# A clustered attention whose loop over units is put together in twos

## The chip, the cores and the metric

The kernel runs on one core of one Trainium2 chip. The metric is the device time of one execution in microseconds; the number quoted for the kernel before is the median of three runs. A core has a matrix engine (TensorE, PE in the rows; PEld is its loading of weights), a vector engine (VectorE, DVE), a scalar engine (ScalarE, ACT), a general engine (GpSimd, POOL) and an engine that issues DMAs (SyncE, SP). Each takes its instructions in the order in which the program emits them; they meet through semaphores, which the framework derives from the tiles that they read and write.

## The reference

Three stages follow one another. Only the first is touched by the change. It is an attention over B = 2 batches, 8 heads, 768 positions and 64 columns a head, in which a query sees only the keys of its own cluster:

```python
q_assign = np.argmax(np.einsum('bhsd,hcd->bhsc', q_n, c_n), axis=-1)
k_assign = np.argmax(np.einsum('bhsd,hcd->bhsc', k_n, c_n), axis=-1)
mask = q_assign[:, :, :, None] == k_assign[:, :, None, :]
scores = scale * np.matmul(q, k.transpose(0, 1, 3, 2))
scores = np.where(mask, scores, -1000000000.0)
scores = scores - np.max(scores, axis=-1, keepdims=True)
attn = np.exp(scores)
attn = attn / (np.sum(attn, axis=-1, keepdims=True) + 1e-09)
return np.matmul(attn, v).astype(np.float32)
```

Then comes a mixture of 8 experts (each token goes to the one with the largest gate, through two matrices of 512x1024 and 1024x512 with a ReLU between), and last a bilinear layer, `(x @ w_a) * (x @ w_b) @ w_out` with an inner width of 1536.

## The kernel before

**Units.** The attention works on eight pairs of heads, one after the other (`p`, 0 to 7). A pair has 2 x 6 blocks of 128 queries, so twelve units (`NU = 12`), 96 in all. A unit takes 128 queries of one head against all 768 keys. Position m in this document is a unit's place in its pair of heads, 0 to 11.

**What a unit does.** `emit_s` computes its scores: four matmuls (512, 256, 512 and 256 columns) into a PSUM tile of two banks, tag `S`, of which there are two; VectorE then reduces them to the negated row maximum (L464). `emit_exp` has ScalarE take the exponential out of that same PSUM tile and sum the rows (L471). `emit_t` turns the probabilities with TensorE: six transposes of 128x128 (L485), three into each of the two banks of tag `T`; the first three are copied to SBUF by ScalarE (L489), the other three by VectorE (L491). The scores of unit i+2 so wait for the exponential of unit i, and the transposes of a unit for the copies of the unit before it.

**Values.** Each six units give a group whose values are computed by `pv_steps`, a generator: three blocks of four matmuls (L501) into the one bank of tag `O`, one block at every second step; behind the third ScalarE copies the result (L508), and one or two steps later `emit_x` turns it back with three matmuls (L529, tile `xo`) into the one bank of tag `X`, which VectorE reads in four operations, the last of them at L542.

**Preparation of the next pair of heads.** `STEPS` gives steps of class `Prep` a place in the loop. All their matmuls use the same single bank of tag `X`, so the next of them waits until the copies out of the one before are done. By position m: m = 10 turns the two halves of the raw queries (`turn`, L344, tiles `xq`, each copied out by ScalarE at L320), the first at "10 minus a half", ahead of the unit's transposes, the second behind them; m = 11 and m = 0 turn the keys (`xk`); m = 1 multiplies with the centroids (`sims`, L352, tile `sm`); m = 3 turns the similarities (`best`, L362, tile `st`; two VectorE operations read it); m = 4 makes the one-hot rows; m = 6 (again "minus a half") turns those of the queries and m = 7 those of the keys (`rows`, L384, tiles `otq` and `otk` with the pair's number; each is copied out by two ScalarE casts at L319 and two VectorE casts at L324).

**The loop.** One iteration i emits, on every engine in this order: scores of unit i, the steps of the values and then the steps planned at i minus a half, transposes of unit i-2 (`LAG = 2`), exponential of unit i, the steps planned at i. Nothing reorders them afterwards. Two iterations in a row put these blocks on TensorE: scores, values, transposes, scores, transposes, with the blocks of `X` between them.

Of the kernel before, what the change touches and what calls it, by code (L numbers as in the profile page):

```python
# [29 lines left out]
def cluster_attention__then__moe__then__bilinear_kernel(  # L30
# [183 lines left out]
    pairs = [(b, hp) for b in range(B) for hp in range(HP)]  # L214
# [5 lines left out]
    def load(p, names):  # L220
        b, hp = pairs[p]
        ts = loaded.setdefault(p, {})
        for src, nm in ((q, "qn"), (k, "kn"), (v, "vn")):
            if nm not in names:
                continue
            if nm == "vn":
                t = ap.tile([128, 2, NT, D], F32, tag=nm, name=f"{nm}{p}", bufs=2)
                nc.sync.dma_start(
                    out=t.rearrange("p h t d -> p h (t d)"),
                    in_=src[b, 2 * hp:2 * hp + 2].rearrange("h (p t) d -> p h (t d)", t=NT),  # L230
                )
            else:
                t = ap.tile([128, NT * 2 * D], F32, tag=nm, name=f"{nm}{p}", bufs=2)
                if p == 0:
                    t = t.rearrange("p (h t d) -> p h t d", h=2, t=NT)
                    nc.sync.dma_start(
                        out=t.rearrange("p h t d -> p h (t d)"),
                        in_=src[b, 2 * hp:2 * hp + 2].rearrange("h (p t) d -> p h (t d)", t=NT),
                    )
                    ts[nm] = t  # L240
                    continue
                t = t.rearrange("p (t h d) -> p t h d", t=NT, h=2)
                for h in range(2):
                    nc.sync.dma_start(
                        out=t[:, :, h, :],
                        in_=src[b, 2 * hp + h].rearrange("(p t) d -> p t d", t=NT),
                    )
            ts[nm] = t
# [204 lines left out]
    def emit_s(u):  # L453
        p, g, h, j = units[u]
        s, t = p % 2, NG * g + j
        if (g, h, j) == (0, 0, 0):
            sums[p] = ap.tile([128, NT, 2], F32, tag="sums", name=f"sums{p}", bufs=2)
        sc = ps.tile([128, 1024], F32, tag="S", name=f"s{u}", bufs=2)
        for i in range(2):
            w = qs[s, h][:, i, 128 * t:128 * t + 128]  # L460
            for c0, c1 in ((0, 512), (512, S)):
                nc.tensor.matmul(sc[:, c0:c1], lhsT=w, rhs=ks[s, h][:, i, c0:c1], start=(i == 0), stop=(i == 1))  # L462
        nm = ap.tile([128, 1], F32, tag="nm", name=f"nm{u}", bufs=3)
        nc.vector.tensor_reduce(out=nm, in_=sc[:, 0:S], axis=AX.X, op=ALU.max, negate=True)  # L464
        return sc, nm

    def emit_exp(u, sc, nm):
        p, g, h, j = units[u]
        pr = ap.tile([128, S], F32, tag="prob", name=f"pr{u}", bufs=3)
        t = NG * g + j  # L470
        nc.scalar.activation(out=pr, in_=sc[:, 0:S], func=AF.Exp, bias=nm, scale=1.0,  # L471
                             accum_out=sums[p][:, t, h:h + 1])
        prob[u] = pr

    def emit_t(u):
        p, g, h, j = units[u]
        pr = prob.pop(u)
        if (p, g, h) not in pt_t:
            pt_t[p, g, h] = ap.tile([128, NT, GN], F32, tag=f"pt{h}", name=f"pt{u}", bufs=2)
        pt = pt_t[p, g, h]  # L480
        for i in range(2):
            x = ps.tile([128, 512], F32, tag="T", name=f"t{u}{i}", bufs=2)
            for n in range(3):
                kb = 3 * i + n
                nc.tensor.transpose(x[:, 128 * n:128 * n + 128], pr[:, 128 * kb:128 * kb + 128], ident)  # L485
            dst = pt[:, 3 * i:3 * i + 3, 128 * j:128 * j + 128]
            src = x[:, 0:GN].rearrange("p (n c) -> p n c", n=3)
            if i == 0 or u >= len(units) - 2:
                nc.scalar.copy(out=dst, in_=src)  # L489
            else:  # L490
                nc.vector.tensor_copy(dst, src)  # L491

    def pv_steps(p, g, j0=0, nj=NG, tags=("O", "X"), per=1, spread=False):


        vn = loaded[p]["vn"]
        n = 128 * nj
        o = ps.tile([128, 512], F32, tag=tags[0], name=f"o{p}{g}{j0}")
        for kb in range(NT):
            for h in range(2):  # L500
                nc.tensor.matmul(o[64 * h:64 * h + 64, 0:n], lhsT=vn[:, h, kb, :],  # L501
                                 rhs=pt_t[p, g, h][:, kb, 128 * j0:128 * j0 + n],
                                 start=(kb == 0), stop=(kb == NT - 1))
            if kb < NT - 1 and kb % per == per - 1:
                for _ in range(per if spread else 1):
                    yield
        ot = ap.tile([128, GN], F32, tag="ot", name=f"ot{p}{g}{j0}", bufs=2)
        nc.scalar.copy(out=ot[:, 0:n], in_=o[:, 0:n])  # L508
        t0 = NG * g + j0
        sm = ap.tile([128, NG, 2], F32, tag="sm", name=f"sm{p}{g}{j0}", bufs=2)  # L510
        nc.vector.tensor_scalar(out=sm[:, 0:nj], in0=sums[p][:, t0:t0 + nj, :], scalar1=1e-9, scalar2=None, op0=ALU.add)
        nc.vector.reciprocal(out=sm[:, 0:nj], in_=sm[:, 0:nj])
        yield
        if spread:
            yield
        if g == 1 and p < LAST - 1:
            yield
        emit_x(p, t0, nj, ot, sm, tags[1])
        yield
# [264 lines left out]
    NU = 12  # L784
    LAG = 2
# [43 lines left out]
    cq, ck = p0.rows("q", "T", 2), p0.rows("k", "O", 1)  # L829
# [73 lines left out]
    end = NU * len(pairs)  # L903
# [33 lines left out]
                             stop=(t == NP - 1 and d % 2 == 1 and i == 1), skip_group_check=True)  # L937

    pvs = []
    for i in range(end + LAG):  # L940
        if i < end:
            sc_nm = emit_s(i)
            if i == 0:
                cq((1,))
                ck((1,))
            if i % NU == 1 and i // NU + 2 < len(pairs):
                load(i // NU + 2, ("qn", "kn"))
            if i % NU == 6 and i // NU + 1 < len(pairs):
                load(i // NU + 1, ("vn",))
        for st in pvs[::-1]:  # L950
            next(st, 0)
        for f in plan.get(i - 0.5, ()):
            f()
        if i == end - 1:
            next(tails[0])
        if i >= end - 1:
            next(r1[0])
        if i == end + 1:
            nc.sync.dma_start(out=x0, in_=xs[0:W].rearrange("(a p) d -> p a d", p=128))
        if i == end:  # L960
            next(tails[0])
            next(tails[1])
            next(r1[1])
        if i == end + 1:
            next(r1[1])
            next(tails[1])
            next(r1[2])
        if i >= LAG:
            emit_t(i - LAG)
        if i < end:  # L970
            emit_exp(i, *sc_nm)
        if i >= LAG:
            p, g, h, j = units[i - LAG]
            if (h, j) == (1, NG - 1) and (p, g) != (LAST, 1):
                last = (p, g) == (LAST, 0)
                pvs.append(pv_steps(p, g, per=3 if last else 2, spread=not last))
                pvs = pvs[-2:]
        for f in plan.get(i, ()):
            f()
        if i == end - 2:  # L980
            next(r1[0])
    next(tails[2])
    next(r1[2])
    place_mm(0, 0)
# [486 lines left out]
```

## Time and profile before

| | |
|---|---|
| median of three runs | 783.31 us (782.85 to 784.54) |
| time of the profiled execution | 783.25 us |
| its span, first to last instruction | 781.1 us |
| mean granted TensorE clock | 0.994 of 2.4 GHz |
| TensorE busy | 761.6 us, 98% of the span |
| VectorE, ScalarE, GpSimd busy | 67%, 46%, 20% |

"Busy" counts an instruction from its start to its modelled end, and matmuls overlap: how long TensorE really takes over a block of instructions is read from the start of one block to the start of the next. Below, a block has its letter in the tile that it writes: `s` scores, `t` transposes, `o` values, `xo`, `xq`, `xk`, `sm`, `st`, `ot5q` and `ot5k` the others. A row merges the instructions of a block (x6: six), its first number is the start of the first, its second the time to the modelled end of the last. A row of the view of windows has the stretch, its length, then the busy time and number of instructions of PE, PEld, DVE, ACT and POOL, the granted clock, the busy share of the DMA engines and the GB/s that they moved.

### The profile page before, as it was taken

Reading aid. Unit: us, or ns where it says so; the run is one execution under the profiler, and the core shown is the slowest. Engines: PE = TensorE matmul, PEld = TensorE weight load, DVE = VectorE, ACT = ScalarE, POOL = GpSimd, SP = SyncE. Lnnn points to the kernel's source line nnn. Section 1 sums busy time; section 2 is a strip of 40 time slices with the busy share of each in tenths; the row PEclk is TensorE's granted clock in tenths of the full one; section 3 lists DMA queues with packets and bytes.
Section 4 is the critical chain, followed back from the end, with each engine's and each line's share of the span. In section 5 each row is a group of like instructions: output and inputs, shape, how many; then the busy total and the mean of one; then the engine's idle time right before and its main releaser. Section 6 shows DMA issues by size and latency. Waiting matters only on the chain. (4 is left out here: it accounts for less than half of the span.)

```text
span 781.1 us, 12589 instructions
## 1 busy us (share of the span) xinstructions
PE 761.6 (98%) x4731; PEld 629.9 (81%) x4731; DVE 523.2 (67%) x947; ACT 355.6 (46%) x677; POOL 156.9 (20%) x164
## 2 busy tenths in 40 slices
PE   9999999999999999999999998999999999999996
PEld 8676676665766789998999997888888888888885
DVE  5867868778687778877686686766456765625323
ACT  6767666675666447547575432323132121210100
POOL 7623221415110410000007000211212112102011
PEclk9999999999999999999999999999999999999999
DMA  6685955737410168858789854322222220001011
GB/s 144 143 192 180 277 134 117 170 92 198 108 49 1 43 215 272 267 173 270 255 275 158 229 166 111 111 79 81 81 55 82 56 80 0 1 1 55 0 55 54
DMA packets 76302, 98.17 MB, mean 126 GB/s; under 512 B 28368, under 2 KB 49360, under 8 KB 76240
## 3 DMA queue, kind: packets, MB, share of 16 engines
q1 hardware_dynamic: 73792, 91.01, 42.2%
q0 software_dynamic: 2304, 6.31, 2.2%
q8 instruction: 38, 0.62, 0.4%
q14 instruction: 24, 0.20, 0.1%
q10 hardware_dynamic: 144, 0.03, 0.0%
HBM read 70.32 MB, written 10.50 MB: 103 GB/s over the span
## 5 line engine op out<-in xcount | busy, mean ns | idle before, releaser
L1408 PE MATMUL ab<-yh,hi 128*128 128x512 f32 x288 | 113.0, 392 | 0.0
L1408 PE MATMUL ab<-yh,lo 128*128 128x512 f32 x288 | 112.6, 391 | 0.0
L1415 DVE TENSOR_TENSOR ga<-ga,ab 128x512 f32<-128x512 f32 x36 | 24.7, 686 | 127.8 <-PE ab L1408 102.1
L464 DVE TENSOR_REDUCE nm<-s 128x1 f32<-128x768 f32 x96 | 91.5, 953 | 18.1 <-PE s L462 14.0
L145 DVE TENSOR_TENSOR lo<-raw,hi 128x1024 fp32r<-128x1024 f32 x70 | 84.8, 1223 | 22.4 <-ACT hi L139 21.7
L471 ACT ACTIVATE pr<-s,nm 128x768 f32<-128x768 f32 x96 | 87.0, 906 | 18.4 <-DVE nm L464 17.9
L462 PE MATMUL s<-ks,qs 128*128 128x512 f32 (+1 forms) x384 | 91.6, 361 | 0.3 <-ACT pr L471 0.3
L1414 ACT COPY ga<-ab 128x512 f32<-128x512 f32 x36 | 21.1, 586 | 151.9 <-PE ab L1408 151.9
L485 PE MATMUL t<-ident,pr 128*128 128x128 f32 x576 | 82.8, 277 | 3.8 <-DVE pt L491 2.2
L485 PEld LDWEIGHTS t<-ident,pr 128*128 128x128 f32 x576 | 64.6, 141 | 25.1 <-issue 10.8
L139 ACT CAST hi<-raw 128x1024 fp32r<-128x1024 f32 x70 | 72.2, 1048 | 17.4 <-DMA raw<-in_moe_w 17.3
L145 POOL TENSOR_TENSOR lo<-tmp,hi 128x512 fp32r<-128x512 f32 x28 | 38.2, 1365 | 204.6 <-ACT hi L139 204.6
L1408 PE MATMUL ab<-yl,hi 128*128 128x512 f32 x288 | 77.0, 389 | 0.0
L501 PE MATMUL o<-pt,vn 128*64 128x384 f32 (+1 forms) x432 | 74.5, 468 | 0.0
L491 DVE COPY pt<-t 128x384 f32<-128x384 f32 x94 | 51.8, 551 | 27.2 <-PE t L485 27.0
L489 ACT COPY pt<-t 128x384 f32<-128x384 f32 x98 | 46.7, 478 | 46.5 <-PE t L485 46.0
L462 PEld LDWEIGHTS s<-ks,qs 128*128 128x128 f32 x384 | 58.5, 190 | 9.6 <-issue 4.4
L1127 PE MATMUL y<-hh,hi 128*128 128x256 f32 x224 | 63.8, 285 | 0.0
L1408 PEld LDWEIGHTS ab<-yh,hi 128*128 128x128 f32 x288 | 54.5, 189 | 11.4
L1408 PEld LDWEIGHTS ab<-yh,lo 128*128 128x128 f32 x288 | 54.5, 189 | 11.3
L1408 PEld LDWEIGHTS ab<-yl,hi 128*128 128x128 f32 x288 | 54.1, 188 | 11.2
L1127 PE MATMUL y<-hh,lo 128*128 128x256 f32 x224 | 62.9, 281 | 0.0
(328 smaller groups left out, 1543.4 us busy)
## 6 DMA issues: line engine op xcount, KB each, us to landing
raw<-in_moe_w SPq DMA_DIRECT2D x72, 512.0 KB, 4.8
raw<-in_moe_w_a SPq DMA_DIRECT2D x12, 512.0 KB, 3.7
raw<-in_moe_w_b SPq DMA_DIRECT2D x12, 512.0 KB, 3.7
raw<-in_moe_w_out SPq DMA_DIRECT2D x12, 512.0 KB, 3.4
qs<-hiq SPq DMA_DIRECT2D x14, 384.0 KB, 4.8
ks<-hik SPq DMA_DIRECT2D x28, 192.0 KB, 4.8
xs<-zero SPq DMA_DIRECT2D x8, 512.0 KB, 5.5
xw<-xs SPq DMA_DIRECT2D x14, 256.0 KB, 5.0
```

Source lines behind the costliest of these rows:

```text
L139: nc.scalar.copy(out=hi, in_=raw)
L145: eng.tensor_tensor(out=lo, in0=raw, in1=hi.bitcast(F32), op=ALU.subtract)
L462: nc.tensor.matmul(sc[:, c0:c1], lhsT=w, rhs=ks[s, h][:, i, c0:c1], start=(i == 0), stop=(i == 1))
L464: nc.vector.tensor_reduce(out=nm, in_=sc[:, 0:S], axis=AX.X, op=ALU.max, negate=True)
L471: nc.scalar.activation(out=pr, in_=sc[:, 0:S], func=AF.Exp, bias=nm, scale=1.0, accum_out=sums[p][:, t, h:h + 1])
L485: nc.tensor.transpose(x[:, 128 * n:128 * n + 128], pr[:, 128 * kb:128 * kb + 128], ident)
L489: nc.scalar.copy(out=dst, in_=src)
L491: nc.vector.tensor_copy(dst, src)
L501: nc.tensor.matmul(o[64 * h:64 * h + 64, 0:n], lhsT=vn[:, h, kb, :], rhs=pt_t[p, g, h][:, kb, 128 * j0:128 * j0 + n], start=(kb == 0), sto ...
L1127: nc.tensor.matmul(y[:, d, 0:n], lhsT=a_[:, fb % 2, 128 * d:128 * d + 128], rhs=b_[:, 0:n], start=(fb == 0 and d % 2 == 0 and i == 0), sto ...
L1408: nc.tensor.matmul(p_, lhsT=a_[:, d, f0:f0 + 128], rhs=b_[d], start=(i == 0), stop=(i == len(seq) - 1))
L1415: nc.vector.tensor_tensor(out=ga, in0=ga, in1=ab[1], op=ALU.mult)
```

## The change

From iteration 4 up to iteration 83, two iterations i (even) and i+1 are emitted together: scores of i, scores of i+1, exponential of i, transposes of i-2, the values of step i with the steps planned at i minus a half, the steps planned at i, exponential of i+1, the values of step i+1, transposes of i-1, the steps planned at i+1. The other iterations (0 to 3 and 84 to 97) are as they were, but for the transposes and the exponential, which are in functions of their own now. No instruction is added or taken away, no tile gets another size or another number of buffers.

```diff
@@ -937,20 +937,27 @@
                              stop=(t == NP - 1 and d % 2 == 1 and i == 1), skip_group_check=True)
 
     pvs = []
-    for i in range(end + LAG):
-        if i < end:
-            sc_nm = emit_s(i)
-            if i == 0:
-                cq((1,))
-                ck((1,))
-            if i % NU == 1 and i // NU + 2 < len(pairs):
-                load(i // NU + 2, ("qn", "kn"))
-            if i % NU == 6 and i // NU + 1 < len(pairs):
-                load(i // NU + 1, ("vn",))
+    sc = {}
+
+    def do_s(i):
+        if i >= end:
+            return
+        sc[i] = emit_s(i)
+        if i == 0:
+            cq((1,))
+            ck((1,))
+        if i % NU == 1 and i // NU + 2 < len(pairs):
+            load(i // NU + 2, ("qn", "kn"))
+        if i % NU == 6 and i // NU + 1 < len(pairs):
+            load(i // NU + 1, ("vn",))
+
+    def do_pv(i):
         for st in pvs[::-1]:
             next(st, 0)
         for f in plan.get(i - 0.5, ()):
             f()
+
+    def do_tails(i):
         if i == end - 1:
             next(tails[0])
         if i >= end - 1:
@@ -965,20 +972,50 @@
             next(r1[1])
             next(tails[1])
             next(r1[2])
+
+    def do_t(i):
         if i >= LAG:
             emit_t(i - LAG)
+
+    def do_exp(i):
         if i < end:
-            emit_exp(i, *sc_nm)
+            emit_exp(i, *sc.pop(i))
+
+    def do_end(i):
         if i >= LAG:
             p, g, h, j = units[i - LAG]
             if (h, j) == (1, NG - 1) and (p, g) != (LAST, 1):
                 last = (p, g) == (LAST, 0)
                 pvs.append(pv_steps(p, g, per=3 if last else 2, spread=not last))
-                pvs = pvs[-2:]
+                del pvs[:-2]
         for f in plan.get(i, ()):
             f()
         if i == end - 2:
             next(r1[0])
+
+    i = 0
+    while i < end + LAG:
+        if 2 * LAG <= i < end - NU and i % 2 == 0:
+
+            do_s(i)
+            do_s(i + 1)
+            do_exp(i)
+            do_t(i)
+            do_pv(i)
+            do_end(i)
+            do_exp(i + 1)
+            do_pv(i + 1)
+            do_t(i + 1)
+            do_end(i + 1)
+            i += 2
+            continue
+        do_s(i)
+        do_pv(i)
+        do_tails(i)
+        do_t(i)
+        do_exp(i)
+        do_end(i)
+        i += 1
     next(tails[2])
     next(r1[2])
     place_mm(0, 0)
```

On TensorE, around m = 10 of one pair of heads (`xq`, `xk`: the raw queries and keys of the next pair; `t`, `s`: transposes and scores of a unit), the kernel before has

```order
L344 MATMUL xq_1697<-ident,qn_1421 128x128 x3
L485 MATMUL t_1702<-ident,pr_1654 128x128 x3
L485 MATMUL t_1707<-ident,pr_1654 128x128 x3
L344 MATMUL xq_1714<-ident,qn_1421 128x128 x3
L462 MATMUL s_1719<-ks_102,qs_101 128x512
...
L485 MATMUL t_1727<-ident,pr_1682 128x128 x3
L485 MATMUL t_1732<-ident,pr_1682 128x128 x3
L344 MATMUL xk_1739<-ident,kn_1424 128x128 x3
```

and the changed kernel

```order
L501 MATMUL o_1658<-pt_1464,vn_1197 64x384
L344 MATMUL xq_1716<-ident,qn_1387 128x128 x3
L344 MATMUL xq_1721<-ident,qn_1387 128x128 x3
L485 MATMUL t_1729<-ident,pr_1663 128x128 x3
L485 MATMUL t_1734<-ident,pr_1663 128x128 x3
L344 MATMUL xk_1739<-ident,kn_1390 128x128 x3
```

The transposes of one unit no longer stand between the two halves of the queries, and between the second half and the keys only one unit's transposes are left, without scores.

On TensorE, around m = 2 and 3 of the next pair of heads (`xo`: the values turned back; `st`: the similarities turned), the kernel before has

```order
L529 MATMUL xo_1834<-iw,ot_1758 128x144 x3
L485 MATMUL t_1844<-ident,pr_1773 128x128 x3
L485 MATMUL t_1849<-ident,pr_1773 128x128 x3
L462 MATMUL s_1861<-ks_98,qs_97 128x512
...
L485 MATMUL t_1868<-ident,pr_1811 128x128 x3
L485 MATMUL t_1873<-ident,pr_1811 128x128 x3
L362 MATMUL st_1880<-ident,sim_1818 128x128 x3
```

and the changed kernel

```order
L529 MATMUL xo_1854<-iw,ot_1596 128x144 x3
L485 MATMUL t_1870<-ident,pr_1801 128x128 x3
L485 MATMUL t_1875<-ident,pr_1801 128x128 x3
L362 MATMUL st_1880<-ident,sim_1818 128x128 x3
```

A block of scores and a block of transposes that stood between the two uses of the bank of tag `X` now stand ahead of the first.

On TensorE, around m = 6 and 7 (`ot4q`, `ot4k`: the one-hot rows of the queries and of the keys), the kernel before has

```order
L384 MATMUL ot4q<-ident,ohp 128x128 x3
L485 MATMUL t_1590<-ident,pr_1538 128x128 x3
L485 MATMUL t_1595<-ident,pr_1538 128x128 x3
L462 MATMUL s_1604<-ks_100,qs_99 128x512
...
L485 MATMUL t_1611<-ident,pr_1561 128x128 x3
L485 MATMUL t_1616<-ident,pr_1561 128x128 x3
L384 MATMUL ot4k<-ident,ohp 128x128 x3
```

and the changed kernel

```order
L384 MATMUL ot4q<-ident,ohp 128x128 x3
L485 MATMUL t_1613<-ident,pr_1550 128x128 x3
L485 MATMUL t_1618<-ident,pr_1550 128x128 x3
L384 MATMUL ot4k<-ident,ohp 128x128 x3
L462 MATMUL s_1631<-ks_100,qs_99 128x512
```

Here too one unit's scores and one unit's transposes have left the stretch between two uses of the bank.

## Rows read from the trace of the kernel before

**Rows 1.** TensorE, instructions in order of time: twelve units of the attention.

```profile
131.44 0.95 PE L462 MATMUL s<-ks,qs 128*128 128x512 f32 x4
...
133.76 0.55 PE L344 MATMUL xq<-ident,qn 128*128 128x128 f32 x3
134.15 0.82 PE L485 MATMUL t<-ident,pr 128*128 128x128 f32 x6
134.94 0.55 PE L344 MATMUL xq<-ident,qn 128*128 128x128 f32 x3
...
136.92 0.95 PE L462 MATMUL s<-ks,qs 128*128 128x512 f32 x4
...
140.97 0.82 PE L485 MATMUL t<-ident,pr 128*128 128x128 f32 x6
141.72 0.52 PE L352 MATMUL sm<-rawq,cblk 128*32 128x384 f32 x2
...
142.50 0.96 PE L462 MATMUL s<-ks,qs 128*128 128x512 f32 x4
...
144.84 1.00 PE L529 MATMUL xo<-iw,ot 128*128 128x144 f32 x6
145.68 0.82 PE L485 MATMUL t<-ident,pr 128*128 128x128 f32 x6
...
147.98 0.49 PE L362 MATMUL st<-ident,sim 128*128 128x128 f32 x3
148.23 0.95 PE L462 MATMUL s<-ks,qs 128*128 128x512 f32 x4
149.11 1.51 PE L501 MATMUL o<-pt,vn 128*64 128x384 f32 x8
150.55 0.87 PE L485 MATMUL t<-ident,pr 128*128 128x128 f32 x6
151.18 0.95 PE L462 MATMUL s<-ks,qs 128*128 128x512 f32 x4
151.96 0.82 PE L485 MATMUL t<-ident,pr 128*128 128x128 f32 x6
152.56 0.97 PE L462 MATMUL s<-ks,qs 128*128 128x512 f32 x4
...
158.10 0.94 PE L462 MATMUL s<-ks,qs 128*128 128x512 f32 x4
...
163.13 0.95 PE L462 MATMUL s<-ks,qs 128*128 128x512 f32 x4
```

**Rows 2.** TensorE, in order of time: the end of one block of scores.

```profile
247.16 0.52 PE L462 MATMUL s<-ks,qs 128*128 128x512 f32 x2
247.39 0.28 PE L462 MATMUL s<-ks,qs 128*128 128x256 f32 x1
247.51 0.27 PE L485 MATMUL t<-ident,pr 128*128 128x128 f32 x1
```

**Rows 3.** VectorE, instructions in order of time, in the same twelve units.

```profile
143.57 0.96 DVE L464 TENSOR_REDUCE nm<-s 128x1 f32<-128x768 f32 x1 [0.91 <-PE s L462]
...
146.53 0.55 DVE L542 TENSOR_TENSOR x<-xo,sm 128x384 f32<-128x384 f32 x1
...
149.84 0.95 DVE L464 TENSOR_REDUCE nm<-s 128x1 f32<-128x768 f32 x1
...
155.70 1.13 DVE L324 CAST qs<-ot5q 32x384 fp32r<-32x384 f32 x2
```

**Rows 4.** ScalarE, instructions in order of time, in the same twelve units.

```profile
134.39 0.49 ACT L320 ACTIVATE rawq<-xq 128x384 f32<-128x384 f32 x1 [1.63 <-issue]
...
137.28 0.90 ACT L471 ACTIVATE pr<-s,nm 128x768 f32<-128x768 f32 x1 [0.25 <-DVE nm L464]
```

**Rows 5.** Busy time, clock and DMA in two stretches of the attention (the view of windows).

```profile
188.00:191.00 3.00, 1.32 (x9) 0.77 (x8) 2.89 (x6) 1.93 (x5) 2.52 (x3) 1.00 0.83 220
192.00:195.00 3.00, 3.00 (x10) 0.87 (x9) 2.00 (x3) 1.39 (x4) 2.23 (x3) 0.50 0.75 285
```

## The prediction

> **What bounds the kernel now.** I read the page's busy shares first: TensorE is busy for 98% of the span, the other engines for 67% at most. The attention is one stretch of that, so I then read TensorE alone, in order of time, over twelve units, that is over one full turn of everything that the loop does for a pair of heads [rows 1]. I name two units that the change puts together by a letter: A is m = 0 and 1, B is 2 and 3, and so on to F, 10 and 11. The starts of their first scores are the frame [rows 1]: F 131.44, A 136.92, B 142.50, C 148.23, D 152.56, E 158.10, the next F 163.13. So before, A takes 5.58 us, B 5.73, C 4.33, D 5.54, E 5.03, F 5.48, together 31.69.
>
> The reader is to see that these are almost nothing but TensorE's own steps. C has no block of preparation: scores to values 0.88, values to transposes 1.44, transposes to scores 0.63, scores to transposes 0.78, transposes to scores 0.60, sum 4.33 [rows 1]. Any gain must come from cheaper passages between such blocks, any loss from waits that their new order makes.
>
> **Prices of the new order.** Nothing is added or removed, so each pair of units is a chain of the same blocks. The passages that it keeps have rows [rows 1]: scores to transposes 0.78, values to what follows 1.44, `xo` to transposes 0.84, `xq` to transposes 0.39, `sm` to scores 0.78, `st` to scores 0.25 (for `xk` and `otk`, also three transposes, the same), transposes to scores 0.60 or 0.63. Two passages are new.
>
> Scores to scores. Inside a block a matmul of 512 columns holds the next off for 0.23 and one of 256 for 0.12 [rows 2], so a block in a stream takes 2 x 0.35 = 0.70; one entered from transposes and left to them takes 0.78. I take 0.78 + 0.70 = 1.48 for two blocks up to the transposes; the bounds are 1.40 and 1.56. The Trainium skill ("TensorE: Matmul & The Clock Gate", section "Back-to-back issue gap") gives a gap of N/2.4 ns plus 2.5 ns for single matmuls. By that rule two blocks would take 1.30 by estimate, 0.18 less in each pair of units but C, and the time forecast below would be about 791 instead of 797; the rows, 0.23 and 0.12 against its 0.216 and 0.109, decide for 1.48.
>
> Transposes to values. Nearest is transposes to `sm`, which also writes a part of the columns: 140.97 to 141.72, 0.75 [rows 1]. Below it lies transposes to scores, 0.60; above it scores to values, 0.88. I take 0.75.
>
> So every pair of units reaches the block behind its values at 1.48 + 0.75 + 1.44 = 3.67 us. From there the waits decide.
>
> **The chain of the other engines.** The reduction starts 1.07 behind the first scores (142.50 to 143.57) and lasts 0.96 [rows 1, 3]; the exponential starts as it ends and holds ScalarE for 0.90 [rows 4]. A copy by ScalarE lasts 0.49, and TensorE writes the freed bank 0.06 after its end (134.39 + 0.49 = 134.88, then 134.94) [rows 1, 4]. So the first exponential runs from 2.03 to 2.93, a copy to 3.42, the second exponential to 4.32. Where ScalarE has more to copy between them it ends later: in D behind casts (from 4.30, for 1.13 if they take what VectorE's take) at 6.33, in F behind the second `xq`'s copy (4.85 + 0.63 + 0.49) at 6.87. The scores that need it come 0.78 into the next pair of units, after 5.4 at the earliest, in D after 6.52 and in F after 7.06 (lengths below). So it is hidden by the transposes and values, by 0.2 only in D and F; what it were late beyond that would add to the time in full.
>
> **The pairs of units one by one.**
> - A: `xk` at 3.67, its transposes 0.39 later, `sm` another 0.75 later (4.81); `sm` needs `xk` copied: 3.67 + 0.63 (134.39 less 133.76) + 0.49 + 0.06 = 4.85. With 0.78 to the scores, 5.63. Change +0.05.
> - B: `xo` at 3.67. VectorE has read it 2.24 later (144.84 to 146.53 + 0.55) [rows 1, 3]. Before, `st` came 3.14 after `xo`, behind scores and transposes of a unit. Now TensorE is there at 3.67 + 0.84 + 0.75 = 5.26 and waits for 3.67 + 2.24 + 0.06 = 5.97. Scores 0.25 later: 6.22, +0.49.
> - C: behind `st` VectorE does `best`'s two operations before it can reduce; from `st` to that reduction it is 1.86 (147.98 to 149.84) [rows 1, 3]. `st` now stands 0.25 before C, so C's reduction starts at 1.61 instead of 1.07, its exponential at 2.57, the copy of its first transposes is over at 2.57 + 0.90 + 0.49 = 3.96, and the second transposes, which write that bank and could start at 3.67, start at 4.02. Plus 0.63: 4.65, +0.32.
> - D: `otq` at 3.67; it can be read 0.63 later, VectorE's two casts take 1.13 [rows 3], so `otk` may go at 3.67 + 0.63 + 1.13 + 0.06 = 5.49, where TensorE is ready at 3.67 + 0.39 + 0.75 = 4.81. 5.49 + 0.25 = 5.74, +0.20 (less than the wait of 0.68, as D waits before too).
> - E: 3.67 + 0.84 + 0.60 = 5.11, +0.08.
> - F: the second `xq` follows the first on the same bank. The row shows what that costs at the least: 133.76 to 134.94, 1.18, filled with transposes before, empty now [rows 1]. The keys then wait for the second copy, another 1.18. 3.67 + 1.18 + 1.18 + 0.25 = 6.28, +0.80. Queued behind the waiting `xq` are the transposes, and behind its copy on ScalarE the second exponential.
>
> Sum 33.63 for twelve units, +1.94. The change covers units 4 to 83: six full turns (A to F), 11.6 us, and C to F of the first pair of heads. The same four give 1.40 there; its first units have no values yet, so second transposes wait for the copy right behind the first, which I add at 0.6 and round to 2.0, an estimate. Behind the attention everything starts when it ends, so the 13.6 us stay. Against the profiled execution's own 783.25 that makes 796.9; it stands within 0.1 us of the median of the runs.
>
> **Rivals.**
> - *The passages win (faster).* If all new waits were covered, B would lose 0.71, C 0.35, D 0.68, F 0.83 and A 0.04 of its length, 2.61 of a turn's 33.63, which leaves 31.02, 0.67 under 31.69. Over 6.67 turns that is 4.5 us, 778.8; with transposes at 0.60 to their follower instead of 0.75 it is nearer 776. It is decided where the new waits add up to less than 0.67 a turn. Against it: F's wait alone is larger, and its 1.18 is a measured row.
> - *Part of the waits is covered.* If B and C do not wait, as when VectorE read `xo` 0.7 us sooner, 1.06 a turn goes and the time is about 790. For it: VectorE is a third idle. Against it: `xo`'s reads start on arrival.
> - *The clock falls.* Before, it did once in the attention: TensorE was busy 1.32 of 3.00 us, and then got 0.50 of the clock for the next stretch [rows 5], which is the lower of its two levels, 1.2 GHz. That costs half of those 3.00 us, 1.5. One such fall a turn would give 797 + 6.67 x 1.5 = 807. The Trainium skill ("TensorE: Matmul & The Clock Gate", section "A second HAM failure mode: psum-queue depth-cycling") says that frequent short idling between groups of matmuls that cycle through PSUM banks can make the clock swing; by that rule this order invites it. Against it: the new waits are 0.4 to 0.8 each, with several us of work between.
> - *No change.* The waits come to just the saved passages.
>
> **Numbers.** Forecast 0.60, its own range 793 to 802; part covered 0.13 (787 to 792); clock 0.12 (803 to 811); faster 0.10; no change 0.05. The unknown prices move the sum by 5 pairs of units x 6.67: transposes to values by -5.0 to +4.3, scores to scores by -2.7 to +2.7. From 787 to 807 both fit, and the cases left out hold about 0.2. A change under 0.2%, 1.6 us, is no change that a measurement here can tell. Faster 0.10, same 0.05, slower 0.85.
>
> **What would show it.** The turn of twelve units should last about 33.6 us. The second `xq` should start 1.18 behind the first and name ScalarE's copy as what it waited for; `st` should wait for VectorE's L542 and come 2.3 after `xo`; `otk` should wait for the casts, 1.8 after `otq`; second scores should start 0.78 after the first and never wait for the exponential. If a turn is 31 us, the waits were covered and the forecast is wrong by its sign; if the clock column shows falls, its size is.

## The result and the profile after

The changed kernel takes 794.45 us, median of four runs (793.32 to 795.6), against 783.08 of the kernel before on the same chip: a ratio of 1.0146, with an interval of 1.0121 to 1.0171. It is slower by 1.5%. Forecast were 796.9 us, slower. The profiled execution took 794.75 us, its span is 792.9 (before: 781.1), its mean clock 0.996.

TensorE alone in order of time, changed kernel, one full turn of six pairs of units (start, length to the modelled end, engine, line, operation, tiles, count; in brackets the idle time before and what ended it). It answers to [rows 1]; D starts at 129.57, E at 135.39, F at 140.46, A at 146.76, B at 152.34, C at 158.60, the next D at 162.97.

```profile
129.57 1.66 PE L462 MATMUL s<-ks,qs 128*128 128x512 f32 x8
131.07 0.82 PE L485 MATMUL t<-ident,pr 128*128 128x128 f32 x6
131.81 1.51 PE L501 MATMUL o<-pt,vn 128*64 128x384 f32 x8
133.25 0.55 PE L384 MATMUL ot4q<-ident,ohp 128*128 128x128 f32 x3
...
135.11 0.52 PE L384 MATMUL ot4k<-ident,ohp 128*128 128x128 f32 x3 [0.66 <-DVE qs L324]
135.39 1.64 PE L462 MATMUL s<-ks,qs 128*128 128x512 f32 x8
...
140.46 1.66 PE L462 MATMUL s<-ks,qs 128*128 128x512 f32 x8
...
144.15 0.55 PE L344 MATMUL xq<-ident,qn 128*128 128x128 f32 x3
145.33 0.55 PE L344 MATMUL xq<-ident,qn 128*128 128x128 f32 x3 [0.63 <-ACT rawq L320]
...
146.46 0.55 PE L344 MATMUL xk<-ident,kn 128*128 128x128 f32 x3
146.76 1.63 PE L462 MATMUL s<-ks,qs 128*128 128x512 f32 x8
...
152.34 1.66 PE L462 MATMUL s<-ks,qs 128*128 128x512 f32 x8
...
156.02 1.00 PE L529 MATMUL xo<-iw,ot 128*128 128x144 f32 x6
...
158.32 0.52 PE L362 MATMUL st<-ident,sim 128*128 128x128 f32 x3 [0.64 <-DVE x L542]
158.60 1.65 PE L462 MATMUL s<-ks,qs 128*128 128x512 f32 x8
...
160.83 1.51 PE L501 MATMUL o<-pt,vn 128*64 128x384 f32 x8
162.34 0.87 PE L485 MATMUL t<-ident,pr 128*128 128x128 f32 x6
162.97 1.66 PE L462 MATMUL s<-ks,qs 128*128 128x512 f32 x8
```

The reader is to see three waits in brackets, each ahead of a block that writes the bank of tag `X`; the view names no others in this turn. The turn is 162.97 - 129.57 = 33.40 us, where [rows 1] had 31.69: +1.71, of which the three waits are 0.66 + 0.63 + 0.64 = 1.93. E, which has no wait, takes 5.07, before 5.03: putting two units together is worth nothing there.

The waits of TensorE over the whole execution, grouped by what waited for what (total, number, longest, us), changed kernel:

```profile
PE xq L344 <- ACT rawq L320: 3.8, 6, 0.6
PE st L362 <- DVE x L542: 3.4, 6, 0.6
PE xo L529 <- DVE sel L596: 2.5, 2, 2.1
...
PE s L462 <- ACT pr L471: 1.8, 3, 0.8
...
PE ot7k L384 <- DVE qs L324: 0.7, 1, 0.7
```

`xq` and `st` wait once in every turn, and so do `ot2k` to `ot7k`, each in a row of its own like the last one (`ot2k` with another releaser, `ot6k`, in the routing turn, for 1.0). All three waits for an exponential come from the first pair of heads, one of them (0.3) ahead of the first paired units, where the kernel before has it too.

The clock over the first turn and over the fourth (view of windows, from one `st` to the next: stretch, length, busy time of PE, PEld, DVE, ACT, POOL, granted clock, DMA share, GB/s):

```profile
26.21:58.12 31.91, 27.55 (x176) 19.55 (x174) 20.72 (x36) 19.69 (x44) 9.09 (x12) 0.95 0.65 160
...
124.92:158.32 33.40, 31.47 (x209) 22.00 (x210) 24.22 (x46) 21.08 (x47) 8.97 (x7) 1.00 0.53 124
```

With its new waits a turn keeps the full clock, 1.00 in each of the five behind the first. The turns from `st` to `st` are 31.91, 33.40, 33.40, 33.40, 33.18 and 33.88; before they were 27.99, 31.75, 31.70, 31.68, 31.40 and 35.25. The sixth and longest before, the one with the routing of the tokens and the half clock of [rows 5], became shorter. (Two of the expectations below call it the fifth; they leave the first out.)

### The profile page after: what moved, and what is told of

The parts are those of the page before. It is cut to its first block, busy times and chain, and to the rows that moved or that the text cites. A ratio compares the mean times of both kernels' runs of the same rounds, so it can differ in the third digit from the quotient of the medians.

```text
span 792.9 us, 12634 instructions
## 1 busy us (share of the span) xinstructions
PE 759.2 (96%) x4731; PEld 629.4 (79%) x4731; DVE 521.5 (66%) x947; ACT 352.9 (45%) x677; POOL 156.3 (20%) x164
## 5 line engine op out<-in xcount | busy, mean ns | idle before, releaser
L464 DVE TENSOR_REDUCE nm<-s 128x1 f32<-128x768 f32 x96 | 88.2, 952 | 18.9 <-PE s L462 16.9
L462 PE MATMUL s<-ks,qs 128*128 128x512 f32 (+1 forms) x384 | 82.6, 353 | 1.8 <-ACT pr L471 1.8
L485 PE MATMUL t<-ident,pr 128*128 128x128 f32 x576 | 80.4, 275 | 1.9 <-ACT pt L489 1.7
L485 PEld LDWEIGHTS t<-ident,pr 128*128 128x128 f32 x576 | 66.2, 142 | 11.4 <-ACT pt L489 6.0
L501 PE MATMUL o<-pt,vn 128*64 128x384 f32 (+1 forms) x432 | 72.7, 462 | 0.0
L1164 PE MATMUL y<-hl,hi 128*128 128x256 f32 x224 | 62.8, 280 | 0.0
```

The source lines that it names most:

```text
L1164: nc.tensor.matmul(y[:, d, 0:n], lhsT=a_[:, fb % 2, 128 * d:128 * d + 128], rhs=b_[:, 0:n], start=(fb == 0 and d % 2 == 0 and i == 0), sto ...
```

## The experiments

Each kernel was timed beside the kernel before on the same chip. That one's own median was 777.88, 781.0, 783.25 and 783.58 in the four comparisons, and one chip gave both 781.0 and 783.25, so I compare ratios, each with the kernel before of its own comparison, and lengths inside the attention. "Turn" is the length of the third and fourth turns from `st` to `st`, which agree within 0.1 us in each kernel (before 31.70, changed 33.40).

| kernel | us | ratio to before (95%) | turn |
|---|---|---|---|
| the change | 794.45 | 1.0146 [1.0121, 1.0171] | 33.40 |
| pairs from unit 12 | 787.7 | 1.0115 [1.0087, 1.0144] | 33.40 |
| half steps first | 783.12 | 1.0072 [1.0048, 1.0095] | 32.25 |
| steps of the odd unit late | 792.22 | 1.0190 [1.0158, 1.0222] | 33.64 |
| only C and E paired | 784.32 | 1.0080 [1.0051, 1.0109] | 32.69 |
| only F paired | 788.88 | 1.0113 [1.0084, 1.0142] | 33.19 |
| half first and odd late, from 12 | 787.83 | 1.0079 [1.0055, 1.0103] | 33.00 |
| the same from 4 | 788.84 | 1.0100 [1.0077, 1.0122] | 33.00 |
| `xo` in the other bank | 793.29 | 1.0130 [1.0101, 1.0159] | 33.40 |
| the change, routing later | 794.37 | 1.0152 [1.0124, 1.0180] | 33.44 |
| before, routing later | 778.58 | 0.9969 [0.9954, 0.9985] | 31.70 |
| four repairs together | 784.0 | 1.0013 [0.9994, 1.0031] | 32.24 |
| the same, copy ahead of the exponential | 780.24 | 0.9959 [0.9943, 0.9975] | 31.48 |

**The theory** is that of the forecast: the turn is longer by the waits on the bank of tag `X`, whose uses have lost the blocks between them. The main rival is that the waits are only where the time shows, and that an order without them would wait elsewhere, or be long by its passages.

**Half steps first.** The steps planned at "i minus a half" are called by a function of their own, ahead of the unit's transposes, so that a unit's transposes stand between the two `xq`, and between `otq` and `otk`, as before.

```diff
...
             do_exp(i)
+            do_half(i)
             do_t(i)
             do_pv(i)
             do_end(i)
             do_exp(i + 1)
             do_pv(i + 1)
+            do_half(i + 1)
             do_t(i + 1)
...
```

> In a pair of units the steps planned at i minus a half go ahead of the transposes of unit i-2 instead of behind the values, so that transposes and values stand between the two xq, and between otq and otk. Theory of the waits on the bank of tag X: F loses its 0.79, D about 0.5 of its wait, 1.3 a turn, 8.6 in all, about 786. Rival: ScalarE and VectorE are the bound by then, and the wait comes back on the exponential or on the copies of the transposes: 792 to 795.

The turn fell by 1.15 to 32.25. F is 5.45 (changed 6.30, before 5.48), and D 5.52 (changed 5.82, before 5.54), where a wait moved. TensorE of this kernel in order of time, the end of D:

```profile
130.47 0.87 PE L485 MATMUL t<-ident,pr 128*128 128x128 f32 x6 [0.48 <-ACT pt L489]
131.18 0.49 PE L384 MATMUL ot4k<-ident,ohp 128*128 128x128 f32 x3
```

`otk` waits no more, but the second transposes wait for ScalarE's copy. So the theory holds for F in full, for D in part. What is left over the 31.70 of before, 0.55, is B with the wait of `st`, which this edit does not touch.

**Steps of the odd unit late.** What is planned at i+1 is put behind the next pair's scores and first exponential. This gives `st`, `otk` and the keys the distance that they lost.

```diff
             do_exp(i)
+            while owed:
+                do_end(owed.pop())
...
             do_t(i + 1)
-            do_end(i + 1)
+            owed.append(i + 1)
```

> The steps planned at the odd unit of a pair go behind the scores and the first exponential of the next pair of units, so that st and otk come after another two blocks of scores. Theory of the waits on the bank of tag X: B loses its 0.64 and D its 0.66, 1.3 a turn, 8.7 in all, about 786. Rival as for the other: the wait comes back elsewhere, 792 to 795.

`st` and `otk` did not wait, and yet the turn became 33.64, longer than in the change. TensorE in order of time, the two blocks of scores with which E begins:

```profile
132.65 0.94 PE L462 MATMUL s<-ks,qs 128*128 128x512 f32 x4
134.38 0.97 PE L462 MATMUL s<-ks,qs 128*128 128x512 f32 x4 [0.78 <-ACT pr L471]
```

Without the wait ahead of `otk` the second scores of E come early, and ScalarE has not finished the exponential that reads their PSUM tile. Of the 1.30 that the two waits had, 0.78 came back here as a wait for the next thing that was late. The rest came back without a wait that the view names, presumably as passages of the moved blocks; that was not measured by itself. The rival has this one.

**Both together,** from unit 12 and from unit 4 on.

> Both moves at once (half steps first, odd unit's steps behind the next scores) and pairing from unit 12. Theory: all waits on the bank of tag X are gone, a turn takes 31.0 by the forecast's passages, six turns 4 us less than before, about 779. Rival, that ScalarE and VectorE then bind (the second exponential): 784 or more.

> The same, but pairing from unit 4 as in the change. Theory: 5 us more than with pairing from unit 12 if the first part's loss is the second transposes' wait for the copy and the fall of the clock behind it, about 784; if those came from the bank of tag X, the same as with pairing from unit 12.

The turn is 33.00 in both, where 31.0 was expected: in D the second transposes wait 1.19 for ScalarE's copy, which stands in its queue behind the exponential and two casts of `otq`. TensorE and ScalarE of the first of the two kernels:

```profile
129.65 0.87 PE L485 MATMUL t<-ident,pr 128*128 128x128 f32 x6 [1.19 <-ACT pt L489]
```

```profile
127.13 0.90 ACT L471 ACTIVATE pr<-s,nm 128x768 f32<-128x768 f32 x1 [2.53 <-DVE nm L464]
...
128.14 0.95 ACT L319 CAST qs<-ot4q 32x384 fp32r<-32x384 f32 x2
129.12 0.48 ACT L489 COPY pt<-t 128x384 f32<-128x384 f32 x1
```

The reader is to see that ScalarE stood idle for 2.53 ahead of an exponential that waited for VectorE, with the copy queued behind it. Pairing the first pair of heads too costs 1.0 here, from the first `st` to the last (211.69 against 210.66), and not the 5 that one theory gave; the wait of 1.71 for ScalarE's copy in the change's first pair (below) is not among the waits of the kernel from 4, but its `ot1q` waits 1.70 where it waited 0.74.

**`xo` in the other bank.** The `xo` of a pair of heads' first group is written one step earlier, into the bank of tag `O` (its values are copied out by then), so that `st` no longer follows it on one bank.

```diff
-        if spread:
+        if spread and g == 1:
             yield
...
-        emit_x(p, t0, nj, ot, sm, tags[1])
+        emit_x(p, t0, nj, ot, sm, tags[0] if spread and g == 0 else tags[1])
```

> The changed kernel, but the values of the first half of a pair of heads are turned back one unit earlier (m = 1) and into the bank of tag O, which is free between its copy and the next values. Theory of the bank of tag X: st no longer waits for the reads of xo; B falls from 6.26 to about 4.7, A rises from 5.58 to about 6.7 (xo's own 0.84 and some 0.3 until the values are copied), a turn 32.9 instead of 33.4, 3.3 us less than the change in all, ratio about 1.010. Rival, that VectorE's late reductions in C take it back: 1.014.

The wait of `st` is gone, and the turn is 33.40 all the same (the second turn is 33.04). `xo` now stands in A, which is 6.70 long, where it was 5.58; B is 4.99 with a wait of 0.26 of its transposes for ScalarE's copy; C is 4.51. A wait of 0.64 removed came back as passages of the moved block and as waits for ScalarE.

**Only some pairs.** Pairing is left to C and E, or to F alone, the other units as before.

```diff
-        if 2 * LAG <= i < end - NU and i % 2 == 0:
+        if NU <= i < end - NU and i % NU in (4, 8):
```

(For F the set is only 10.)

> Only C and E (units 4 and 5, 8 and 9 of a pair of heads, from unit 12 on) are put together; in them no use of the bank of tag X follows another closely. Theory: the passages alone are worth nothing, +0.04 for each by the changed kernel's trace against the one before, so +0.5 in all, 783.6. Rival, that two blocks of scores in a row cost something of themselves (1.0 a turn or more): 789 and above. Rival, that the order saves where no wait eats it: 780 or less.

> Only F (units 10 and 11, from unit 12 on) is put together: the two xq stand one behind the other, all else as before. Theory: +0.82 for each of six, 4.9, about 788. Rival, that a wait at one place is taken back by slack in the next units: 784 to 785.

Both missed: +1.0 and +1.5 a turn. The first is the price that the rival gave, but not for its reason. A pair behind a single unit has a wait of its own at its entry. TensorE in order of time, C of the first kernel, then F of the second:

```profile
118.28 0.94 PE L462 MATMUL s<-ks,qs 128*128 128x512 f32 x4
119.53 0.98 PE L462 MATMUL s<-ks,qs 128*128 128x512 f32 x4 [0.31 <-ACT pr L471]
```

```profile
133.68 0.95 PE L462 MATMUL s<-ks,qs 128*128 128x512 f32 x4
135.06 0.97 PE L462 MATMUL s<-ks,qs 128*128 128x512 f32 x4 [0.43 <-ACT pr L471]
```

The second scores need the PSUM tile of unit i-1, whose exponential a single iteration emits behind its transposes. From scores to scores it is 1.25 and 1.38 instead of the 0.70 forecast. The second `xq` of F waits 0.63 as in the change; the pair alone costs more than inside a row of pairs.

**Pairs from unit 12,** that is without the first pair of heads.

```diff
-        if 2 * LAG <= i < end - NU and i % 2 == 0:
+        if NU <= i < end - NU and i % 2 == 0:
```

> Pairing begins at unit 12 instead of 4; the first pair of heads is as before. Theory of the waits: the changed kernel's trace has units 4 to 12 in 23.76 us (23.02 to 46.78) where the kernel before has 18.78, so this loses that 5.0 and takes about 789.5. The forecast's own term for this part, 2.0, would give 792.4. If the loss sat only in the later turns, 794.4.

From the first `st` to the last it is 211.06 (10.34 to 221.40) instead of 215.51 (9.87 to 225.38): leaving the first pair of heads as it was gives back 4.4, where the forecast had put 2.0 on it. The start at unit 12 pays an entry wait of its own (0.46 ahead of the second scores at 43.52). The ratios differ by 0.3%, with intervals that overlap, so the trace carries this.

**Routing later.** The kernel before, with the second half of the tokens' routing planned four units later, and the change with the same.

```diff
-    steps_at(mid + 16, r0, NT + 1)
+    steps_at(mid + 20, r0, NT + 1)
```

> The kernel before with the routing of the first batch (its rank matmuls and six scatters by GpSimd) planned four units later. Theory: in the fifth turn of the kernel before VectorE's operation at L511 takes 1.51 us beside a scatter, TensorE waits 1.7 for it and then has half its clock, so that turn takes 35.25 where the others take 31.7; the changed kernel has 33.88 there because the waits fall elsewhere. Without that the kernel before takes 3.5 less, about 779.6. Rival: the later scatters meet the same operations at another place, 783.

> The changed kernel with the routing planned four units later, as was done to the kernel before (0.997 of its time). Theory: the kernel before loses 3.5 to the stall and the fall of the clock in its fifth turn, which the changed kernel does not have (33.88 against its other turns' 33.4), so here only some 0.5 goes: ratio 1.014 to the kernel before, and 1.017 to the kernel before with later routing. Rival, that both lose the same: 1.011.

The kernel before gains 0.3%: its long turn of 35.25 is 32.21, at the full clock. The changed kernel gains nothing: 34.06 where it was 33.88. So the change had already lost most of that stall by where it shifted the routing, and against the kernel before with the later routing it is 1.0152 / 0.9969 = 1.018, a quotient from two comparisons. L511 did not run beside a scatter, as the expectation has it, but beside another GpSimd operation (last section).

**The repairs together:** pairs from 12, half steps first, `xo` in the other bank, later routing; and then the same with the first transposes of a pair emitted ahead of its first exponential, so that ScalarE's copy of them no longer stands behind it. The second edit, against the kernel of the four repairs:

```diff
-            do_exp(i)
             do_half(i)
             do_t(i)
+            do_exp(i)
             do_pv(i)
```

> All that helped: pairing from unit 12, half steps first, xo of the first half in the bank of tag O, routing four units later. Theory: turns of about 31.75 (32.25 less 0.5), no first-part loss, no fall of the clock at the routing: as the kernel before with later routing, ratio 0.997 to 1.000. That is, with the new waits taken out the order itself is worth nothing. Rival, that the saved passages show once the waits are gone: 0.992 or less.

> The combined kernel with one more exchange: in a pair of units the transposes of unit i-2 are emitted ahead of the first exponential, so that ScalarE copies them out before that exponential, as in the kernel before, and the second transposes find their bank free. Theory: the waits of transposes for ScalarE's copies that are left in the combined kernel (0.48 in D, 0.26 in B, 0.15 in C of a turn of 32.25) go, a turn takes about 31.4, 0.3 less than before; with the later routing the ratio is 0.994. Rival: the later exponential now holds up the second scores, and the turn stays at 32 or more, ratio 0.999 or above.

The four repairs leave waits of the transposes for ScalarE's copy (0.48 in D, 0.26 in B, 0.15 in C), a turn of 32.24 and a ratio of 1.0013. With the copy put ahead they are gone. TensorE of the last kernel, D:

```profile
121.25 1.66 PE L462 MATMUL s<-ks,qs 128*128 128x512 f32 x8
...
125.27 1.21 PE L485 MATMUL t<-ident,pr 128*128 128x128 f32 x6
...
126.56 1.66 PE L462 MATMUL s<-ks,qs 128*128 128x512 f32 x8
```

D is 5.31, and the turn 31.48 against 31.70: that is what pairing is worth in an order whose turns have no wait that the view names, 0.2 us a turn. All of it stands in D, which is 5.54 in the kernel before and has a wait there; transposes of D, kernel before:

```profile
157.00 1.01 PE L485 MATMUL t<-ident,pr 128*128 128x128 f32 x6 [0.21 <-ACT pt L489]
```

A and B together are 11.34 (before 11.31, changed 11.84), C 4.28, E 5.10, F 5.44: with the waits on the bank gone the loss is gone, and outside D nothing is won. Nor is D quite free: its second transposes take 1.04 up to `otk` where they took 0.71 in "half steps first". The last kernel also loses 1.1 in its first turn (29.17 against 28.04), so its ratio of 0.9959 is that of the later routing alone (0.9969) within the intervals. The last kernel and the kernel before with later routing both beat the one before; that the pairing adds to the later routing is not shown.

## Why the prediction was right

**Its sign and mechanism.** The mechanism was as forecast: passages that bring nothing, and waits on one bank. Its marks in the trace came as named: second `xq` 1.18 behind the first for ScalarE's copy, `st` 2.30 behind `xo` for L542, `otk` 1.86 behind `otq` for the casts. By taking the missing distances back, the first experiment showed the cause for `xq`, and for `otk` as far as ScalarE let it. For `st` it took the last kernel: `xo` in the other bank alone removed its wait and not its cost, and only with ScalarE's copies put right as well were A and B back at 11.34. In the steady turns no scores waited for an exponential, as forecast.

**The prices.** Two blocks of scores up to the transposes took 1.47 to 1.51, forecast 1.48. The estimate by the Trainium skill ("TensorE: Matmul & The Clock Gate", section "Back-to-back issue gap"), 1.30, does not agree with it. Transposes to values took 0.74, forecast 0.75. Pair by pair:

| | A | B | C | D | E | F | turn |
|---|---|---|---|---|---|---|---|
| before | 5.58 | 5.73 | 4.33 | 5.54 | 5.03 | 5.48 | 31.69 |
| forecast | 5.63 | 6.22 | 4.65 | 5.74 | 5.11 | 6.28 | 33.63 |
| measured | 5.58 | 6.26 | 4.37 | 5.82 | 5.07 | 6.30 | 33.40 |

**C was mis-sized.** The forecast took 1.86 from `st` to the reduction behind `best` from [rows 1, 3]. VectorE in order of time, changed kernel:

```profile
158.88 0.56 DVE L367 TENSOR_REDUCE mx<-st 128x24 f32<-128x384 f32 x1 [0.24 <-PE st L362]
...
159.94 1.81 DVE L464 TENSOR_REDUCE nm<-s 128x1 f32<-128x768 f32 x2
```

`st` had waited, so VectorE's copy was over before it and `best` began at once: 158.32 to 159.94 is 1.62. The copy of the first transposes was so over in time, and the second ones start 1.51 behind the values instead of 1.44: 0.07 of a wait, not 0.35. A term taken from a row of the old order held an instruction that the new order puts elsewhere.

**The first pair of heads was mis-sized:** from scores of unit 4 to those of unit 12 it is 23.76 (23.02 to 46.78) instead of 18.78 before, +5.0, forecast +2.0. TensorE in order of time there, changed kernel, then VectorE:

```profile
24.75 0.97 PE L462 MATMUL s<-ks,qs 128*128 128x512 f32 x4 [0.80 <-ACT pr L471]
...
30.64 0.55 PE L384 MATMUL ot1q<-ident,ohp 128*128 128x128 f32 x3 [0.74 <-DVE ohp L375]
32.90 1.54 PE L485 MATMUL t<-ident,pr 128*128 128x128 f32 x6 [1.71 <-ACT pt L489]
34.10 2.44 PE L462 MATMUL s<-ks,qs 128*128 128x512 f32 x8
36.38 0.81 PE L485 MATMUL t<-ident,pr 128*128 128x128 f32 x6
...
41.18 0.97 PE L462 MATMUL s<-ks,qs 128*128 128x512 f32 x4 [0.71 <-ACT pr L471]
```

```profile
29.44 0.55 DVE L373 TENSOR_REDUCE mx<-oh 128x24 f32<-128x384 f32 x1 [0.67 <-POOL oh L369]
...
30.50 1.82 DVE L464 TENSOR_REDUCE nm<-s 128x1 f32<-128x768 f32 x2
```

The four waits are 3.96 together; 34.10 to 36.38 is 2.28 where the same blocks take 1.50, at a lower clock (below). Here the one-hot rows stand close behind `st`, and VectorE's operation waits for GpSimd with the pair's reduction behind it, so exponential and copy come late. The forecast said that the second scores never wait for the exponential; here they did twice. It had put the entry at 0.6, an estimate for which it showed no row of this stretch.

**The routing turn was not in the forecast.** It added +1.94 there too; measured is 33.88 - 35.25 = -1.4, 3.3 less.

**One F too many.** The forecast put F's +0.80 on six full turns and on the first pair of heads. The last F has no `xq`, since no further pair of heads is prepared there: it takes 4.32 (240.92 to 245.24), before 4.33. That is 0.8 less.

**The sum.** From scores of unit 4 to those of unit 84 it is +11.4 by the trace (222.22 against 210.82). The forecast had 13.6; +3.0 for the first pair of heads, -3.3 for the routing turn, -0.8 for the last F and -1.1 for the other turns, chiefly C, make 11.4. The changed execution had come to unit 4 0.28 sooner, so the loop ends 11.1 later. The 11.8 of the span contain a wait of 2.1 near the attention's end (below), and about 1.1 regained behind it. So the size came out nearly right in part by luck: errors of opposite signs met.

**The rivals.** "The passages win" fell with E, 5.07 without a wait, and with the last kernel: an order nearly free of waits saves 0.2 a turn, not 0.67. (With the cheaper transposes the forecast set this rival "nearer 776"; by the -5.0 that it gives for that price it is 773.8.) That rival took the waits out and left the order alone; an order that avoids them puts blocks of `X` back between scores and transposes, and moves `xo`, and so has other passages. "Part of the waits is covered" was true of C alone. "The clock falls" once a turn did not come: 1.00 in each of the five turns behind the first, with three waits of about 0.65 in each. The Trainium skill's rule ("TensorE: Matmul & The Clock Gate", section "A second HAM failure mode: psum-queue depth-cycling") did not take hold at waits of this size; what the clock did in the first pair of heads is no test of it, as it came behind one wait of 1.71.

## What to carry to other kernels

Blocks that seem to be only work are also the distance between two uses of a single buffer. Before putting iterations together, list the uses of every buffer that there is once, and measure what is left between them against the time that the readers take; where that is too little, the gain in passages must be larger than the wait. A wait that is taken away from one engine is often found again on the next one's queue: look there for an instruction that stands behind one that waits, and change that order too.

## What the runs showed of the hardware

**A small operation that ends when GpSimd's does.** The routing turn of before was long because VectorE's L511, on 128x6 values, took 1.51 us. VectorE and then GpSimd of the kernel before, then the same two of the kernel before with later routing:

```profile
187.08 1.51 DVE L511 TENSOR_SCALAR sm<-sums 128x6 f32<-128x6 f32 x1
```

```profile
185.45 1.23 POOL L559 DMA_INDIRECT xs<-x,slot  x1 [0.55 <-PE s L462]
186.72 1.83 POOL L413 TENSOR_TENSOR rawk<-rawk,hik 128x768 fp32r<-128x768 f32 x1
```

```profile
186.61 0.26 DVE L511 TENSOR_SCALAR sm<-sums 128x6 f32<-128x6 f32 x1
```

```profile
185.02 1.82 POOL L413 TENSOR_TENSOR rawk<-rawk,hik 128x768 fp32r<-128x768 f32 x1
```

L511 ends at 188.59 and L413 at 188.55; with the later routing at 186.87 and 186.84. In the change (L511 1.04, L413 from 198.71 for 1.82) the ends are 200.58 and 200.53, and where L511 does not meet L413, as in the change's other turns, it takes 0.16. In four other turns of the kernel before it starts just ahead of L413's end and ends as closely behind it, in one of them at 92.05 (91.80 and 0.25) against 92.03 (90.21 and 1.82). The scatter in GpSimd's queue had pushed L413 1.7 us later, onto L511, and behind L511 stood the casts and a copy for which TensorE waited 1.33. The Trainium skill ("SBUF — State Buffer", section "SBUF: two separate sides") says that GpSimd's operations and some of VectorE's (those in a two-port mode, or with two inputs from SBUF) share a pair of ports, of which the first to start has the whole for its instruction while the other waits; the ends of these rows agree. Which mode L511 ran in no row shows.

**A clock that falls in some executions.** Two windows of the changed kernel in its first pair of heads, and the second of them for the changed kernel with later routing:

```profile
31.00:34.00 3.00, 1.29 (x7) 1.10 (x6) 2.90 (x5) 2.48 (x6) 2.86 (x7) 0.74 0.08 5
34.00:37.00 3.00, 3.00 (x17) 2.66 (x15) 1.73 (x3) 1.36 (x4) 0.61 (x1) 0.69 0.81 221
```

```profile
34.00:37.00 3.00, 3.00 (x22) 2.29 (x22) 2.92 (x5) 2.58 (x8) 1.02 (x1) 1.00 0.66 189
```

With a wait of 1.71 and of 1.72 and the same order up to there the granted clock fell (a window's value is a mean over its stretch; at its lowest it was 0.50, the lower of its two levels) in the one execution and not in the other, where the stretch before has 1.00 too; the first turn was 31.91 and 30.61. "Half steps first" has the same wait and fell too (0.65 and 0.79 in these windows), `xo` in the other bank has it and did not. What decides it these runs don't show.

**A wait that stays open.** In the change, and in four of the experiments (the change with later routing, `xo` in the other bank, both kernels of the repairs together), an `xo` near the end of the attention waits 2.1 to 2.3 us for VectorE's L596; in the others and before the longest such wait is 0.4. It is no part of the forecast's mechanism. L596 is itself late: in the change it starts at 281.98, although the matmul whose result it reads (L594) ended at 280.16, and ScalarE's copy of the values (L508) starts only at 281.21 for matmuls that ended at 279.29. What held both was not tried.
